# Moving the block differences of a two-stage MLP from GpSimd to VectorE, and giving the last token group its former first-stage order

## The chip, the cores and the metric

The kernel runs on one core of one Trainium2 chip. The metric is device time in microseconds (us), the median of three runs. Beside the runs there is one profiled execution, and every row of a trace in this document is from such an execution. The engines are PE (TensorE, matmul), PEld (its weight loads), DVE (VectorE), ACT (ScalarE), POOL (GpSimd) and SP (SyncE, which here issues nearly all DMAs).

## What is computed

```
scores = scale * q @ k.T - log(S)              # batch 8, 12 heads, S = 448, head size 64
attn   = 1 / (1 + exp(-scores))
x      = (attn @ v) as tokens x 768            # 3584 tokens
h      = x @ w_in                              # 768 x 2048
out    = relu(h)**2 @ w_out                    # 2048 x 768
```

Everything is float32 at the interface. The MLP behind the attention is the part that matters here.

## The kernel before

**Attention** runs first (to about 245 us of the span) and writes x to memory. The MLP then takes the 3584 tokens in four groups, g = 0 to 3. Groups 0, 1 and 2 hold 512 columns in each of two halves, group 3 holds 256 in each of two halves.

**Seven products.** Each group has two stages: the first multiplies by `w_in`, the second by `w_out`. Each matrix product is made from 2x2 blocks with seven block products instead of eight, so both operands are first combined by additions. The products are numbered 1 to 7. In the second stage they run one after the other in the order 1, 2, 6, 7, 5, 4, 3 (`ORDER`), each over eight positions i. In the first stage single steps (product, position) alternate, in an order that is a list: `LEAD` with the rest of `ROUNDS` behind it, then `TAIL`.

**Split operands.** A float32 operand is split into a high part (ACT copies it to the narrower type: line 379, tile names ending in h) and a low part (DVE subtracts the high part from the operand: line 381, names ending in l). A product of two split operands takes three matmuls: high x high, high x low, low x high. So ACT and then DVE stand before each operand of PE. Weights are loaded by SP into a pool of seven tiles (`w`), and a load waits until PE has used up the tile that it overwrites. A third of the last group's first-stage weights use other tiles (`spare`).

**Quartered products.** In groups 1 and 2 the products 2, 7 and 4 of the second stage (`TWICE`) are taken apart once more by the same scheme. For that each raw operand of 128x1024 (four pieces, j = 0 to 3, each with four blocks of 128x256) needs four *block differences*, t1, t3, t2, t4 (`differences_of`, lines 838 to 854). t2 needs t1, and t4 needs t2. For products 7 and 4 they overwrite the operand in place, for product 2 they go to a tile named d. They too are split: tiles d...h by ACT and d...l by DVE, and the split is placed `SPLIT_AFTER` steps later in the program. PE uses them in matmuls that write the banks oq (line 887).

**The order on each engine** is made by a scheduler when the program is built; each engine then runs its own list strictly in that order. An instruction that waits holds up all that stand behind it on its engine. PE does not pass over a matmul whose operand is late.

**The last group.** In group 3 the first stage takes the same list as the other groups (`STEPS[0]`), with about half the time for each step, because a step has 256 columns instead of 512. The operands of its products 7, 5, 3 and 4 are made during its own first steps:

```
EARLY_X = {0: (7,), 1: (5,), 3: (3,), 5: ("t4",), 6: (4,)}
...
            if m == 0 and 0 < g:
                for name in EARLY_X.get(at - sequence.index((g, 0, *order_of(g, 0)[0])), ()):
                    next_x[g - 1][name]()
```

In the first stage one PSUM bank takes the products 1, 6, 5 and 3 of a position one on top of the other (chain a). After product 1 and after product 6 ACT copies the bank (`snap`, line 754; tiles s1, s2), and the next product of that position must not write before the copy is done.

Of the kernel before, what the change touches and what calls it, by code (L numbers as in the profile page):

```python
# [15 lines left out]
ALU = mybir.AluOpType  # L16
# [12 lines left out]
NG = B // 2  # L29
# [11 lines left out]
NG = len(WIDTHS)  # L41
# [16 lines left out]
ROUNDS = [  # L58
    (n, j)
    for i in range(NI - 2)  # L60
    for n, j in ((1, i), (5, i - 1), (2, i), (6, i), (3, i - 1), (7, i), (4, i - 1))
    if 0 <= j
]
Y, Z = NI - 2, NI - 1
TAIL = [(1, Y), (5, Y - 1), (1, Z), (2, Y), (3, Y - 1), (2, Z), (4, Y - 1), (6, Y), (6, Z), (7, Y), (7, Z)]
TAIL += [(5, Y), (5, Z), (4, Y), (4, Z), (3, Y), (3, Z)]
LEAD = [(1, 0), (2, 0), (1, 1), (2, 1), (6, 0), (7, 0), (6, 1)]
LEAD += [(5, 0), (7, 1), (3, 0), (1, 2), (2, 2), (4, 0)]

STEPS = [LEAD + [s for s in ROUNDS if s not in LEAD] + TAIL]  # L70

BEHIND = {512: [(7, Y), (5, Y), (4, Y), (3, Y)], 256: [(7, Z), (4, Y)]}

# [9 lines left out]
    (3, 0): ("t3",),  # L83
}
EARLY_X = {0: (7,), 1: (5,), 3: (3,), 5: ("t4",), 6: (4,)}

ORDERS = [(n, i) for n in ORDER for i in range(NI)]
LAST = ORDER[-1], -1

TWICE = (2, 7, 4)  # L90
TWICE_IN = (1, 2)
SPLIT_AFTER = 5
Q = WIDE // 2
SUMS_AT = {2: (0, 0), 3: (0, 1), 4: (1, 0), 5: (1, 1), 1: (2, 0), 6: (2, 1), 7: (3, 0)}

# [13 lines left out]
def sigmoid_attention_relu2_mlp(  # L109
# [48 lines left out]
    nc = tc.nc  # L158
# [3 lines left out]
    def flat2(name, dtype=F32):  # L162
        return sb.tile([P, 2 * WIDE], dtype, tag="op2", bufs=N2, name=name)
# [214 lines left out]
    def split_to(hi, lo, raw, later=None):  # L378
        nc.scalar.copy(out=hi, in_=raw)  # L379
        if later is None:  # L380
            nc.vector.tensor_sub(out=lo, in0=raw, in1=hi.bitcast(F32))  # L381
        else:
            later.append(lambda: nc.vector.tensor_sub(out=lo, in0=raw, in1=hi.bitcast(F32)))
# [252 lines left out]

    def order_of(g, m):
        if m == 0:
            return STEPS[0]
        return ORDERS if g < NG - 1 else [*ORDERS[:-NI], LAST]  # L640

    sequence = [(g, m, n, i) for g in range(NG) for m in range(2) for n, i in order_of(g, m)]

    def units_of(g, m, n, i):
# [56 lines left out]
    spare = set()  # L701
    for at_unit, unit in enumerate(units):
        ahead, use = 0, first_use[unit]
        if unit[0] == NG - 1 and use >= sequence.index((NG - 1, 0, *STEPS[0][0])) + 4:
            ahead = 4
            if at_unit % 3 == 0:
                spare.add(unit)
        if at_unit >= READY:
            stream.setdefault(max(use - LOAD_AHEAD - ahead, 0), []).append((fetch, unit))
        if at_unit >= HALVED:  # L710
            stream.setdefault(max(use - HALVE_AHEAD - ahead // 2, 0), []).append((halve, unit))
        if unit[:2] == (0, 1):
            stream.setdefault(use - HALVE_AHEAD + KEEP_AFTER, []).append((keep, unit))
# [98 lines left out]
    def gemm2(g, blocks, operands1):  # L812
# [3 lines left out]
        ops, t2 = {1: operands1}, {}  # L816
# [3 lines left out]
        def operand(n, j):  # L820

            if n == 6:
                t2[j] = blocks_of(f"gt2_{g}_{j}", n_tok)
                nc.vector.tensor_sub(out=t2[j], in0=blocks["22", j], in1=blocks["12", j])
                raw = t2[j]
            elif n == 7:
                raw = blocks["11", j]
                nc.vector.tensor_sub(out=raw, in0=t2[j], in1=raw)
            elif n == 4:
                raw = blocks["21", j]  # L830
                nc.vector.tensor_sub(out=raw, in0=raw, in1=t2[j])
            else:
                raw = blocks[{2: "21", 5: "12", 3: "22"}[n], j]
            ops.setdefault(n, {})[j] = split_or_joint(raw, f"o{n}_{g}_{j}", n_tok)
            if n in twice:
                differences_of(n, j, raw)

        def differences_of(n, j, raw):

            name = f"d{n}_{g}_{j}"  # L840
            flat = raw.rearrange("p k s -> p (k s)")
            to = flat2(name) if n == 2 else flat
            b11, b12, b21, b22 = (flat[:, n * Q : n * Q + Q] for n in range(4))
            t1, t3, t4, t2 = (to[:, n * Q : n * Q + Q] for n in range(4))
            nc.gpsimd.tensor_tensor(out=t1, in0=b12, in1=b11, op=ALU.subtract)  # L845
            nc.gpsimd.tensor_tensor(out=t3, in0=b22, in1=b12, op=ALU.subtract)
            nc.gpsimd.tensor_tensor(out=t2, in0=b22, in1=t1, op=ALU.subtract)  # L847
            nc.gpsimd.tensor_tensor(out=t4, in0=b21, in1=t2, op=ALU.subtract)

            def parts():  # L850
                differences[n, j] = hi, lo = flat2(name + "h", F32R), flat2(name + "l", F32R)
                split_to(hi, lo, to)

            postponed.setdefault(now[0] + SPLIT_AFTER, []).append(parts)

# [181 lines left out]
    def run_steps(begin, end, between):  # L1037
        for at in range(begin, end):
            g, m, n, i = sequence[at]
            now[0] = at  # L1040
            if (m, n, i) == (0, *order_of(g, 0)[0]):
                made[g] = gemm1(g, ops[g])
            if (m, n, i) == (1, *ORDERS[0]):
                step, blocks, operands, done = made[g]
                done()
                second[g] = gemm2(g, blocks, operands)
            (second[g] if m else made[g][0])(n, i)
            for piece in between.get(at, []) + postponed.pop(at, []):
                piece()
            for piece, unit in stream.get(at, ()):  # L1050
                piece(unit)
            if m and g < NG - 1:
                if (n, i) == next(iter(NEXT_X)):
                    ops[g + 1], next_x[g] = x_operands(g + 1)
                for name in NEXT_X.get((n, i), ()):
                    next_x[g][name]()
            if m == 0 and 0 < g:
                for name in EARLY_X.get(at - sequence.index((g, 0, *order_of(g, 0)[0])), ()):
                    next_x[g - 1][name]()

    made, second, next_x, postponed, now = {}, {}, {}, {}, [0]

    with tc.manual_schedule():
# [46 lines left out]
        for n, piece in work:  # L1110
            between.setdefault(n, []).append(piece)
        run_steps(0, len(STEPS[0]), between)
    run_steps(len(STEPS[0]), len(sequence), {})


# [42 lines left out]
```

## Time and profile before

| what | value |
|---|---|
| median of 3 runs (lowest to highest) | 1064.69 us (1063.99 to 1065.31) |
| the profiled execution: its own time | 1063.85 us |
| its span, first to last instruction | 1062.1 us |
| PE busy | 1049.0 us, 99% |
| PEld busy | 819.9 us, 77% |
| DVE busy | 833.2 us, 78% |
| ACT busy | 689.0 us, 65% |
| POOL busy | 235.4 us, 22% |
| mean granted TensorE clock | 0.998 |

The span leaves out a little at both ends, which is why the execution's own time is 1.75 us longer. A share of busy time is a mean over stages that differ. A matmul's end is modelled in the profile, and neighbouring matmuls overlap, so the lost time of PE is better read from where a product starts and ends than from its busy share.

### The profile page before, as it was taken

The page shows a single profiled execution, that of the slowest core. Times are in us where ns is not written, and L with a number is a line of the kernel's source. Part 1 is how long each engine was busy: PE and PEld are TensorE (multiplying, and loading weights), DVE is VectorE, ACT ScalarE, POOL GpSimd, SP SyncE. Part 2 cuts the span into 40 slices and gives each one's busy share as a digit, 9 for nine tenths or more (in the row PEclk, how much of TensorE's full clock was granted, in tenths as well). Part 3 has the DMA queues.
Part 4 walks back from the last instruction along what each step waited for, and adds up shares of the span by engine and source line. Part 5 has one row for each costly group of instructions (what it writes and reads, how often), then busy time and mean ns, then how long its engine had stood idle before and what let it go on. Part 6 is the DMA issues. An engine that isn't in the chain of part 4 may idle for free.

```text
span 1062.1 us, 17197 instructions
## 1 busy us (share of the span) xinstructions
PE 1049.0 (99%) x6418; PEld 819.9 (77%) x6418; DVE 833.2 (78%) x1045; ACT 689.0 (65%) x960; POOL 235.4 (22%) x188
## 2 busy tenths in 40 slices
PE   9999999999999999999999998999999998999998
PEld 4555555557888888888888887888888887889987
DVE  6999998977768899796546788794556788958897
ACT  7998998877667855645444647564445646657873
POOL 1222231300222345300001537300003367200000
PEclk9999999999999999999999999999999999999999
DMA  9999999983666787993335877953337787856662
GB/s 366 404 394 368 337 405 361 326 300 111 214 215 208 242 275 249 326 325 114 97 104 175 275 270 241 350 153 92 89 97 244 240 311 256 264 174 180 204 198 85
DMA packets 121874, 255.93 MB, mean 241 GB/s; under 512 B 11712, under 2 KB 63680, under 8 KB 121792
## 3 DMA queue, kind: packets, MB, share of 16 engines
q1 hardware_dynamic: 121648, 254.79, 70.5%
q8 instruction: 50, 0.82, 0.3%
q14 instruction: 32, 0.26, 0.1%
q10 hardware_dynamic: 144, 0.07, 0.0%
HBM read 193.46 MB, written 61.34 MB: 240 GB/s over the span
## 4 chain that ended last, share of the span: by engine, by line
PE 90%; POOL 4%; DVE 3%; DMA 2%; ACT 1%; issue 0%; SPq 0%; ACTq 0%
PE ha L623 22%; PE oa L623 15%; PE pav L353 11%; PE hb L623 9%; PE sc L322 9%; PE hc L623 5%; PE ob L623 4%; PE oq L887 2%; PE oa L631 2%; PE oc L623 2%; PE sr L338 2%; PE pav L365 2%; POOL g L845 2%; DMA w<-w 1%; POOL g L847 1%; PE ob L631 1%
## 5 line engine op out<-in xcount | busy, mean ns | idle before, releaser
L381 DVE TENSOR_TENSOR w<-w 128x768 fp32r<-128x768 f32 (+1 forms) x164 | 148.9, 915 | 86.9 <-ACT w L379 75.2
L379 ACT CAST w<-w 128x768 fp32r<-128x768 f32 (+1 forms) x165 | 127.4, 781 | 95.7 <-DMA w<-w 85.5
L310 ACT ACTIVATE at<-sc 128x896 f32<-128x896 f32 x144 | 119.2, 941 | 3.0 <-PE sc L322 3.0
L353 PE MATMUL pav<-at,v 64*64 64x448 f32 x1152 | 118.1, 540 | 0.0
L353 PEld LDWEIGHTS pav<-at,v 64*64 64x64 f32 x1152 | 41.6, 133 | 60.8 <-issue 53.3
L212 POOL TENSOR_TENSOR a<-a,f 128x768 int32<-128x768 int32 x24 | 52.9, 2202 | 158.7 <-DVE a L209 82.9
L687 ACT CAST w<-w 128x768 fp32r<-128x768 f32 x56 | 46.7, 834 | 46.3 <-DMA w<-w 33.2
L754 ACT COPY s<-ha 128x512 f32<-128x512 f32 (+1 forms) x64 | 34.0, 533 | 65.2 <-PE ha L623 61.6
L845 POOL TENSOR_TENSOR d<-g 128x256 f32<-128x256 f32 x8 | 9.3, 1166 | 282.6 <-PE ha L623 136.5
L589 DVE TENSOR_TENSOR ql<-x,qh 128x896 fp32r<-128x896 f32 x46 | 67.9, 1516 | 0.0
L322 PE MATMUL sc<-qh 64*128 64x448 f32 x282 | 53.9, 379 | 0.0
L322 PE MATMUL sc<-ql,qh 64*128 64x448 f32 x282 | 51.3, 361 | 0.0
L322 PE MATMUL sc<-qh,ql 64*128 64x448 f32 x282 | 51.2, 360 | 0.0
L375 DVE TENSOR_TENSOR xo<-pav,xo 128x448 f32<-128x448 f32 x48 | 29.5, 621 | 24.5 <-ACT xo L371 24.3
L212 POOL TENSOR_TENSOR b<-b,fd 128x384 int32<-128x384 int32 x16 | 20.4, 1277 | 118.8 <-ACT w L379 56.9
L623 PE MATMUL oa<-o_0h,w 128*128 128x512 f32 x144 | 46.3, 389 | 0.0
L623 PE MATMUL oa<-o_1h,w 128*128 128x512 f32 x144 | 46.3, 389 | 0.0
L623 PE MATMUL oa<-o_2h,w 128*128 128x512 f32 x144 | 46.3, 389 | 0.0
L623 PE MATMUL oa<-o_3h,w 128*128 128x512 f32 x144 | 46.3, 389 | 0.0
L623 PE MATMUL ha<-x_0h,w 128*128 128x512 f32 x128 | 44.8, 390 | 0.0
L623 PE MATMUL ha<-x_2h,w 128*128 128x512 f32 x128 | 44.6, 389 | 0.0
L623 PE MATMUL ha<-x_1h,w 128*128 128x512 f32 x128 | 44.6, 389 | 0.0
(587 smaller groups left out, 3065.3 us busy)
## 6 DMA issues: line engine op xcount, KB each, us to landing
w<-w SPq DMA_DIRECT2D x193, 384.0 KB, 3.6
w<-h SPq DMA_DIRECT2D x56, 384.0 KB, 5.1
x<-qk SPq DMA_DIRECT2D x47, 448.0 KB, 6.3
f<-w_in SPq DMA_DIRECT2D x16, 768.0 KB, 8.6
v<-v SPq DMA_DIRECT2D x24, 448.0 KB, 6.9
xd<-xo SPq DMA_DIRECT2D x48, 224.0 KB, 4.9
h<-w SPq DMA_DIRECT2D x28, 384.0 KB, 4.3
w<-s SPq DMA_DIRECT2D x48, 192.0 KB, 7.3
```

The source lines that it names most:

```text
L212: nc.gpsimd.tensor_tensor(out=wb, in0=wb, in1=t.bitcast(I32)[:, :, 0], op=ALU.add)
L310: nc.scalar.activation(at, sc, AF.Sigmoid, bias=NEG_LOG_S, scale=SCALE)
L322: nc.tensor.matmul(sc[:, j], x[kp][rows, 1, ks], x[qp][rows, 0], start=(n == 0), stop=(n == len(passes) - 1),)
L353: nc.tensor.matmul(sums[columns, h], vt[rows, n % 2 * NT + t, columns], at[t][rows, j], start=(t == 0 and (n % 2, h) != (1, 1)), stop=(t = ...
L379: nc.scalar.copy(out=hi, in_=raw)
L381: nc.vector.tensor_sub(out=lo, in0=raw, in1=hi.bitcast(F32))
L589: nc.vector.tensor_sub(out=xs[n][1], in0=x[n], in1=xs[n][0].bitcast(F32))
L623: nc.tensor.matmul(out, a[:, c], b, start=first and n == 0, stop=last and n == 2, skip_group_check=True)
L631: nc.tensor.matmul(out, w[0][:, c], x, start=first, stop=False, skip_group_check=True)
L687: nc.scalar.copy(out=hi, in_=hi.bitcast(F32))
L754: nc.scalar.copy(out=s, in_=banks[chain, i])
L845: nc.gpsimd.tensor_tensor(out=t1, in0=b12, in1=b11, op=ALU.subtract)
```

## The change

Four things, in one edit. The four block differences are formed by DVE instead of GpSimd. Their split is placed two steps later in the program instead of five. The first stage of group 3 takes the list `ROUNDS + TAIL` (no `LEAD`). The operands of group 3's products 7, 5, 3 and 4 are made during product 3 of group 2's second stage (`LATE_X`) instead of during group 3's first steps.

```
-STEPS = [LEAD + [s for s in ROUNDS if s not in LEAD] + TAIL]
+STEPS = LEAD + [s for s in ROUNDS if s not in LEAD] + TAIL, ROUNDS + TAIL
...
+LATE_X = {(3, 1): (7,), (3, 3): (5,), (3, 5): (3,), (3, 6): ("t4",), (3, 7): (4,)}
...
-SPLIT_AFTER = 5
+SPLIT_AFTER = 2
...
-            return STEPS[0]
+            return STEPS[g == NG - 1]
...
-            nc.gpsimd.tensor_tensor(out=t1, in0=b12, in1=b11, op=ALU.subtract)
-            nc.gpsimd.tensor_tensor(out=t3, in0=b22, in1=b12, op=ALU.subtract)
-            nc.gpsimd.tensor_tensor(out=t2, in0=b22, in1=t1, op=ALU.subtract)
-            nc.gpsimd.tensor_tensor(out=t4, in0=b21, in1=t2, op=ALU.subtract)
+            nc.vector.tensor_sub(out=t1, in0=b12, in1=b11)
+            nc.vector.tensor_sub(out=t3, in0=b22, in1=b12)
+            nc.vector.tensor_sub(out=t2, in0=b22, in1=t1)
+            nc.vector.tensor_sub(out=t4, in0=b21, in1=t2)
...
-            if m == 0 and 0 < g:
+                for name in LATE_X.get((n, i), ()) if g == NG - 2 else ():
+                    next_x[g][name]()
+            if m == 0 and 0 < g < NG - 1:
```

What this does to DVE's list is seen at product 7 of group 1's second stage. Before, from the first split of product 7's operands on (o7 are those splits, d7 the splits of the differences, o5 the splits for product 5; the two digits behind are group and piece j, the last number a tile's own):

```order
L381 TENSOR_TENSOR o7_1_0l_6457<-g11_1_0_5312,o7_1_0h_6456 128x1024
L381 TENSOR_TENSOR o7_1_1l_6492<-g11_1_1_5480,o7_1_1h_6491 128x1024
L381 TENSOR_TENSOR o7_1_2l_6527<-g11_1_2_5699,o7_1_2h_6526 128x1024
L828 TENSOR_TENSOR g11_1_3_5906<-gt2_1_3_6408,g11_1_3_5906 128x1024
L381 TENSOR_TENSOR d7_1_0l_6544<-g11_1_0_5312,d7_1_0h_6543 128x1024
L831 TENSOR_TENSOR g21_1_1_5658<-g21_1_1_5658,gt2_1_1_6330 128x1024
L381 TENSOR_TENSOR o7_1_3l_6568<-g11_1_3_5906,o7_1_3h_6567 128x1024
L381 TENSOR_TENSOR d7_1_1l_6589<-g11_1_1_5480,d7_1_1h_6588 128x1024
L831 TENSOR_TENSOR g21_1_2_5851<-g21_1_2_5851,gt2_1_2_6371 128x1024
L381 TENSOR_TENSOR o5_1_0l_6623<-g12_1_0_5450,o5_1_0h_6622 128x1024
L831 TENSOR_TENSOR g21_1_3_6054<-g21_1_3_6054,gt2_1_3_6408 128x1024
L381 TENSOR_TENSOR d7_1_2l_6633<-g11_1_2_5699,d7_1_2h_6632 128x1024
```

The same place in the changed kernel, from the same split on (its lines count one more; 846 to 849 are the differences):

```order
L382 TENSOR_TENSOR o7_1_0l_6457<-g11_1_0_5312,o7_1_0h_6456 128x1024
L382 TENSOR_TENSOR o7_1_1l_6492<-g11_1_1_5480,o7_1_1h_6491 128x1024
L846 TENSOR_TENSOR g11_1_0_5312<-g11_1_0_5312 128x256
L846 TENSOR_TENSOR g11_1_1_5480<-g11_1_1_5480 128x256
L847 TENSOR_TENSOR g11_1_0_5312<-g11_1_0_5312 128x256
L847 TENSOR_TENSOR g11_1_1_5480<-g11_1_1_5480 128x256
L848 TENSOR_TENSOR g11_1_0_5312<-g11_1_0_5312 128x256
L848 TENSOR_TENSOR g11_1_1_5480<-g11_1_1_5480 128x256
L849 TENSOR_TENSOR g11_1_0_5312<-g11_1_0_5312 128x256
L849 TENSOR_TENSOR g11_1_1_5480<-g11_1_1_5480 128x256
L829 TENSOR_TENSOR g11_1_3_5906<-gt2_1_3_6408,g11_1_3_5906 128x1024
L382 TENSOR_TENSOR d7_1_0l_6500<-g11_1_0_5312,d7_1_0h_6499 128x1024
```

The differences of the pieces 0 and 1 now stand behind the second split, taken in turn. Those of the pieces 2 and 3 follow in the same way after four more splits (o7 and d7) and before the split d7 of piece 2. Three instructions of 128x1024 stand between the splits d7 of the pieces 2 and 3.

The other place is ACT's list where group 3 begins. Before, from the first copy of a bank in group 3 on (s1 and s2 are the copies after products 1 and 6, the digits behind are group and position; w0 are weights of the first stage: group, position, unit; x5 and x3 are operands of group 3):

```order
L754 COPY s1_3_0_9182<-ha_3_0_9172 128x256
L379 CAST x5_3h_9206<-x12_3_8852 128x768
L379 CAST w0_3_2_1_9204<-w0_3_2_1_9204 128x768
L754 COPY s1_3_1_9220<-ha_3_1_9210 128x256
L379 CAST x3_3h_9233<-x22_3_8854 128x768
L379 CAST w0_3_3_0_9262<-w0_3_3_0_9262 128x768
L754 COPY s2_3_0_9246<-ha_3_0_9172 128x256
```

The same place in the changed kernel, again from the first copy of a bank in group 3 on:

```order
L755 COPY s1_3_0_9205<-ha_3_0_9195 128x256
L380 CAST w0_3_2_0h_9168<-w0_3_2_0l_9169 128x768
L380 CAST w0_3_2_1_9219<-w0_3_2_1_9219 128x768
L755 COPY s2_3_0_9230<-ha_3_0_9195 128x256
L755 COPY s7_3_0_9239<-hb_3_0_9232 128x512
L380 CAST w0_3_3_0_9274<-w0_3_3_0_9274 128x768
L755 COPY s1_3_1_9253<-ha_3_1_9243 128x256
L380 CAST w0_3_2_2_9285<-w0_3_2_2_9285 128x768
```

The casts of x5 and x3 are gone from here (they stand earlier). The copy s2 of position 0 now stands behind the cast of `w0_3_2_1` and ahead of that of `w0_3_3_0`, and the copy s1 of position 1 stands behind the cast of `w0_3_3_0`.

## Rows read from the trace of the kernel before

**Rows 1.** The page's chain of waits: shares of the span by engine.

```profile
PE 90%; POOL 4%; DVE 3%; DMA 2%; ACT 1%; issue 0%; SPq 0%; ACTq 0%
```

**Rows 2.** Waits of PE: whom it waited for, total us, times, longest.

```profile
PE oq L887 <- DVE d_2l L381: 2.6, 2, 1.3
PE oq L887 <- ACT d_2h L379: 2.0, 2, 1.0
PE oq L887 <- DVE d_3l L381: 1.8, 2, 0.9
PE ha L623 <- ACT s L754: 1.7, 1, 1.7
...
PE oq L887 <- DVE d_1l L381: 0.6, 1, 0.6
```

**Rows 3.** PE's timeline, first matmuls of products; last: group 3's third step. Start, duration.

```profile
635.97 0.28 PE L887 MATMUL oq<-o_0h,w 128*128 128x256 f32 x1
...
656.19 0.39 PE L623 MATMUL oa<-o_0h,w 128*128 128x512 f32 x1
...
672.51 0.28 PE L887 MATMUL oq<-o_0h,w 128*128 128x256 f32 x1
...
705.24 0.39 PE L623 MATMUL ha<-x_2h,w 128*128 128x512 f32 x1
...
904.25 0.28 PE L887 MATMUL oq<-o_0h,w 128*128 128x256 f32 x1
...
936.17 0.28 PE L623 MATMUL ha<-x_3h,w 128*128 128x256 f32 x1
...
938.29 0.28 PE L623 MATMUL ha<-x_3h,w 128*128 128x256 f32 x1
```

**Rows 4.** Timeline of POOL: first and last of product 7's sixteen differences, group 1.

```profile
626.83 3.93 POOL L845 TENSOR_TENSOR g<-g 128x256 f32<-128x256 f32 x1 [23.37 <-DVE o_0l L381]
...
649.89 0.74 POOL L848 TENSOR_TENSOR g<-g 128x256 f32<-128x256 f32 x1
```

**Rows 5.** Timeline of ACT, product 7: in brackets idle time before, and releaser.

```profile
650.66 1.05 ACT L379 CAST d_3h<-g 128x1024 fp32r<-128x1024 f32 x1 [3.11 <-POOL g L848]
```

**Rows 6.** Timeline of DVE in group 1's second stage.

```profile
623.94 0.41 DVE L906 TENSOR_TENSOR qe<-oq,qe 128x256 f32<-128x256 f32 x1
624.27 0.41 DVE L911 TENSOR_TENSOR q<-q,qt 128x256 f32<-128x256 f32 x1
...
626.67 1.22 DVE L381 TENSOR_TENSOR o_1l<-g,o_1h 128x1024 fp32r<-128x1024 f32 x1
...
640.76 1.75 DVE L831 TENSOR_TENSOR g<-g,gt 128x1024 f32<-128x1024 f32 x1
...
661.30 0.42 DVE L905 TENSOR_TENSOR qt<-oq,qe 128x256 f32<-128x256 f32 x1
661.76 0.42 DVE L906 TENSOR_TENSOR qe<-oq,qe 128x256 f32<-128x256 f32 x1
...
675.66 1.22 DVE L436 TENSOR_TENSOR x<-x,x 128x1024 f32<-128x1024 f32 x1 [4.98 <-DMA x<-xd]
```

**Rows 7.** Windows, group 1's second stage: length; busy of PE, PEld, DVE, ACT, POOL.

```profile
588.00:704.00 116.00, 112.10 (x607) 96.68 (x606) 95.42 (x96) 70.81 (x87) 49.39 (x41) 1.00 0.79 267
```

**Rows 8.** Timeline of ACT at the start of group 3.

```profile
940.14 0.83 ACT L379 CAST w<-w 128x768 fp32r<-128x768 f32 x1 [1.60 <-issue]
...
944.35 0.83 ACT L379 CAST w<-w 128x768 fp32r<-128x768 f32 x1 [2.36 <-DMA w<-w]
945.09 0.37 ACT L754 COPY s<-ha 128x256 f32<-128x256 f32 x1
```

**Rows 9.** Timeline of SP: issue of the transfers that those two casts wait for.

```profile
936.36 0.33 SPq L284 DMA_DIRECT2D w<-w  x1
...
938.48 0.33 SPq L284 DMA_DIRECT2D w<-w  x1
```

**Rows 10.** Windows of 2 us behind: length, five busy times, granted clock, DMA share, GB/s.

```profile
946.00:948.00 2.00, 2.00 (x11) 1.81 (x10) 1.74 (x5) 2.00 (x5) 0.00 (x0) 0.53 0.16 63
948.00:950.00 2.00, 2.00 (x12) 1.90 (x11) 1.98 (x4) 1.18 (x3) 0.00 (x0) 0.61 0.00 0
```

More of the change, by code (lines that the diff above doesn't have):

```diff
@@ L703, in sigmoid_attention_relu2_mlp @@
         ahead, use = 0, first_use[unit]
-        if unit[0] == NG - 1 and use >= sequence.index((NG - 1, 0, *STEPS[0][0])) + 4:
+        if unit[0] == NG - 1 and use >= sequence.index((NG - 1, 0, *STEPS[1][0])) + 4:
             ahead = 4
```

## The prediction

> **What bounds the kernel now.** I read the chain of waits first. PE carries 90% of it, and POOL and DVE the most of what is left [rows 1]. So the kernel is a list of matmuls, and a change gains only what it takes away of PE's standing still. PE's waits say where that is [rows 2]: matmuls into the banks oq, which exist only in quartered products, wait for splits d_h and d_l of the block differences, and one wait of group 3's chain a is for ACT's copy of a bank. A row that counts two times is one wait in group 1 and one in group 2.
>
> How much time this is I take from where products begin, since a matmul's end is modelled [rows 3]. Product 7 of group 1 lasts 656.19 - 635.97 = 20.22 us. For an undisturbed quartered product I use group 2's products 4 and 3, which together last 936.17 - 904.25 = 31.92, and product 5 of group 1 (a plain product, as 3 is), 672.51 - 656.19 = 16.32. That leaves 31.92 - 16.32 = 15.60 for product 4, or 3.90 for each of four pieces. Product 7 therefore loses 20.22 - 15.60 = 4.62. Two groups: 9.24. Products 4 and 3 of group 1 last 705.24 - 672.51 = 32.73, so 0.81 is lost there, where DVE stood 4.98 us before an addition that waited for the DMA of an x tile [rows 6], with the split d_1l behind it in its list. [...] At those clocks the windows do 2 x 0.53 and 2 x 0.61 us of full-speed work, so 0.94 + 0.78 = 1.72 go too. In all 9.24 + 0.81 + 1.7 + 1.72 = 13.5 us stand to be won.
>
> **Why product 7 stalls.** POOL's sixteen differences for it start at 626.83 and end at 649.89 + 0.74 = 650.63, 23.8 us [rows 4]. ACT's cast d_3h has waited 3.11 us when the last one releases it, at 650.66 [rows 5]. Piece 3 is due at 635.97 + 3 x 3.90 = 647.67. PE arrives three to four us before its operand is made, and DVE still has to split it.
>
> **The differences on DVE.** Each quartered product takes 16 instructions of 128x256, 48 in a group, 96 in all. The trace has no such DVE instruction with all three tiles in SBUF, so I bound its price by neighbours of the same shape [rows 6]: independent ones begin 0.33 apart (623.94, 624.27), dependent ones 0.46 apart (661.30, 661.76). The new list takes two pieces in turn, so a result is mostly not needed by the next instruction: I take 0.36, nearer to the lower bound.
>
> Now product 7, rolled forward in the new order. DVE's second split began at 626.67 and lasts 1.22 [rows 6], to 627.9. Behind it: eight differences (2.6 to 3.7), five instructions of 128x1024 (6.1; beside POOL they take up to 1.75, but POOL has no differences any more), eight differences with one long instruction among them (3.8 to 4.9), ACT's cast d_2h (1.05 [rows 5]), then d_2l (1.22). That ends at 642.7 to 644.9, or 641.5 to 643.7 where the long instruction runs during ACT's cast. At 0.36 d_2l is there at about 642, before piece 2 is due (635.97 + 7.80 = 643.8). d_3l comes three long instructions and itself later (4.9), at about 647, just ahead of 647.7, and PE takes the low parts behind the first high ones. At both upper bounds together PE would wait about 1 us. What is late next in that case is DVE's splits o5 of product 5, which have their full product 7 to hide behind. So I give back the whole 4.62 per group.
>
> DVE's load over the second stage: 95.42 of 116 us are busy now [rows 7]. The differences add 48 x 0.33 = 15.8 to 48 x 0.46 = 22.1. Contention given back takes away between 0 and 30% ((1.75 - 1.22) / 1.75 [rows 6]) of POOL's 49.39 us [rows 7], 14.8. So DVE comes to between 96.4 and 117.5, and with 0.36 and half of the contention to 95.4 + 17.3 - 7.4 = 105.3, in a stage of 116 - 4.62 - 0.81 = 110.6. It fits, with 5 us spare; at the unfavourable ends it does not. For the 0.81 I count a full return, as the x operand's DMA is issued ahead of the output stores in the new order and the splits that stand behind it are those of product 3.
>
> [...]
>
> **Two steps later instead of five.** The split is now placed soon behind differences that DVE itself makes, so it waits only for ACT's cast. Cost nothing while DVE has other splits between (it has, three long ones); if that cover is gone, 1.05 us per piece.
>
> **Group 3's start.** Two steps last 938.29 - 936.17 = 2.12 us there [rows 3], one 1.06. Before, ACT's copy s2 of position 0 began at 945.09, right behind a cast that had waited 2.36 for its weights [rows 8], whose transfer SP issued at 938.48 [rows 9], 5.9 us before. In the new list s2 stands behind the cast of w0_3_2_1 instead, the one at 940.14 [rows 8], so it can start at about 941, before it is needed (five steps in, 941.5). What takes the place of that wait: s1 of position 1 now stands behind the cast of w0_3_3_0, and its bank is needed seven steps in, 943.6. With a transfer of 3.8 us (936.36 to 940.14 [rows 8, 9]) from an issue at about 938.5 the cast is there at 942.3, done at 943.1 and the copy (0.37) at 943.4: no wait. With 5.9 us it is 944.4 and some 1.9 us of wait, plus the clock again. The new list holds the following load back longer, so fewer transfers run beside it; I take 0.2. The x operands that leave this place are made beside product 3 of group 2, a plain product of 16.32 us with no differences to make; in the second stage of group 1 ACT is busy 70.81 and DVE 95.42 of 116 us [rows 7], so the room is there, and I count nothing. If it is not, x4 is late, which is used last.
>
> **Sum.** 13.5 - 0.2 = 13.3 us. The profiled execution's own time is 1063.85 (span 1062.1 and 1.75 at its ends); less 13.3 is 1050.55. The median of the runs, 1064.69, is 0.84 above the profiled execution, which gives 1051.4 in its terms. I take 1051.0.
>
> **Rivals.** **(A)** the forecast, 1051.0, own range 1050.0 to 1052.5; 0.58. **(B)** Group 3's wait is only moved, behind the cast of w0_3_3_0 (transfer 5.9 as before): 3.4 us stay, 1054.5. For it: the late transfer of [rows 8, 9]; against: fewer loads beside it. 0.18. **(C)** DVE becomes the bound of product 7 in part: differences at 0.46 and little contention returned. Between 1 us (the roll forward) and 6.9 us (117.5 - 110.6) per group, in the middle 4.6 over both, 1055.6. Against it: POOL's long spans vanish. 0.12. **(D)** Slower: DVE's list puts differences ahead of the splits o...l that PE needs first. A product's sixteen at 0.46 are 7.4 us, in six stages; if half lies bare, 22 us, and the time is 1063.85 - 13.3 + 22 = 1072.5. It decides from 13.3 / 6 = 2.2 us bare per stage on. Against it: product 7's operands o are split a whole product ahead of PE. 0.07. **(E)** No gain, 1064.7: DVE is slowed by as much as POOL was late. For it: a long instruction takes 1.75 instead of 1.22 beside POOL [rows 6], so the two engines share something. Against it: after the change POOL has nothing left to do there. [...] 0.05.
>
> **How the numbers follow.** A measurement of this kernel tells about 0.2%, 2.1 us, from no change. A, B and C are faster by more (0.88), E is the same (0.05), D slower (0.07). The range reaches from A's lower end, less 0.2 for the scatter of runs, over B to a little beyond C's middle, 1049.8 to 1056.0; outside lie D, E and C's far half.
>
> **What would show it.** Right: product 7 of groups 1 and 2 begins 15.6 us ahead of product 5, no oq wait is left, differences on DVE begin 0.33 to 0.46 apart, DVE's long instructions take 1.22 all through, DVE is busy about 105 us of the stage, and the windows at group 3's start have a granted clock of 1.00 with no ha wait. Wrong: oq waits for d_3l (C), an ha wait for s behind a cast of weights (B), or waits for o_l at the beginnings of quartered products (D).

## The result, and the profile after

| | before | changed |
|---|---|---|
| median of the runs (lowest to highest) | 1064.34 us (1062.60 to 1065.31), 4 runs (one more than in the first table) | 1052.79 us (1052.28 to 1053.76), 4 runs |
| the profiled execution's own time | 1063.85 us | 1052.28 us |
| its span | 1062.1 us | 1050.5 us |
| DVE busy; POOL busy | 833.2; 235.4 us | 843.8; 116.9 us |
| mean granted TensorE clock | 0.998 | 1.000 |

The ratio is 0.9894 with a 95% interval of 0.9877 to 0.9912: faster by 1.1%. The forecast was 1051.0 in a range of 1049.8 to 1056.0. In terms of the profiled execution it was 1050.55, and 1052.28 came, so 11.6 of the 13.3 us were won.

PE's waits in the changed kernel, as in [rows 2] (whom it waited for, total us, times, longest):

```profile
PE oa L632 <- DVE o_1j L382: 0.8, 1, 0.8
...
PE ha L624 <- ACT s L755: 0.4, 1, 0.4
```

The four rows of [rows 2] on the banks oq are gone altogether. Group 3's wait for s is 0.4 instead of 1.7, and a wait for o_1j has come that was not there before.

PE's timeline answers to [rows 3]: starts of product 7, 5 and 4 and of the next group's first stage in group 1, the beginning and end of product 7 and the beginning of product 4 in group 2, the start of group 3, and the two matmuls with a wait:

```profile
636.29 0.28 PE L888 MATMUL oq<-o_0h,w 128*128 128x256 f32 x1
...
651.89 0.39 PE L624 MATMUL oa<-o_0h,w 128*128 128x512 f32 x1
...
668.21 0.28 PE L888 MATMUL oq<-o_0h,w 128*128 128x256 f32 x1
...
700.13 0.39 PE L624 MATMUL ha<-x_2h,w 128*128 128x512 f32 x1
...
862.61 0.28 PE L888 MATMUL oq<-o_0h,w 128*128 128x256 f32 x1
...
878.21 0.39 PE L624 MATMUL oa<-o_0h,w 128*128 128x512 f32 x1
...
894.53 0.28 PE L888 MATMUL oq<-o_0h,w 128*128 128x256 f32 x1
...
926.45 0.28 PE L624 MATMUL ha<-x_3h,w 128*128 128x256 f32 x1
...
934.50 0.39 PE L624 MATMUL ha<-x_3h,w 128*128 128x256 f32 x1 [0.43 <-ACT s L755]
...
1039.17 1.33 PE L632 MATMUL oa<-o_1j,w 128*128 128x512 f32 x4 [0.81 <-DVE o_1j L382]
```

Product 7 lasts 651.89 - 636.29 = 15.60 us in group 1 and 878.21 - 862.61 = 15.60 in group 2. Products 4 and 3 last 700.13 - 668.21 = 31.92 in group 1 and 926.45 - 894.53 = 31.92 in group 2, which is the undisturbed length of [rows 3]. The second stage of both groups now runs without a gap.

DVE's timeline in product 7 of group 1: the second split, the first eight of the new differences (L846 to L849) and the two splits that PE had waited for:

```profile
627.29 1.22 DVE L382 TENSOR_TENSOR o_1l<-g,o_1h 128x1024 fp32r<-128x1024 f32 x1
628.43 0.75 DVE L846 TENSOR_TENSOR g<-g 128x256 f32<-128x256 f32 x2
629.10 0.75 DVE L847 TENSOR_TENSOR g<-g 128x256 f32<-128x256 f32 x2
629.77 0.75 DVE L848 TENSOR_TENSOR g<-g 128x256 f32<-128x256 f32 x2
630.44 0.76 DVE L849 TENSOR_TENSOR g<-g 128x256 f32<-128x256 f32 x2
631.12 1.22 DVE L829 TENSOR_TENSOR g<-gt,g 128x1024 f32<-128x1024 f32 x1
...
640.99 1.23 DVE L382 TENSOR_TENSOR d_2l<-g,d_2h 128x1024 fp32r<-128x1024 f32 x1 [0.29 <-ACT d_2h L380]
...
645.54 1.22 DVE L382 TENSOR_TENSOR d_3l<-g,d_3h 128x1024 fp32r<-128x1024 f32 x1
```

Eight differences take from 628.43 to 631.12, 2.69 us, so they begin 0.336 apart. d_2l is ready at 642.22 and d_3l at 646.76. In this execution product 7 begins at 636.29, so the pieces 2 and 3 are due at 644.09 and 647.99: margins of 1.9 and 1.2 us. Windows over group 1's second stage, as in [rows 7]:

```profile
588.00:700.00 112.00, 112.00 (x613) 97.69 (x613) 104.71 (x147) 72.27 (x89) 0.00 (x0) 1.00 0.82 281
```

DVE is busy 104.71 of 112 us, and POOL, 49.39 before, has nothing left to do.

The page's chain of waits, as in [rows 1], and then the piece of that chain behind which the wait for o_1j lies (start, us, what):

```profile
PE 92%; DVE 4%; ACT 1%; DMA 1%; issue 1%; SPq 0%; ACTq 0%; DVEq 0%
```

```profile
1008.53 5.25 DMA w<-w
...
1013.88 0.83 ACT w L380
...
1038.52 0.61 DVE o_1j L382
...
1039.17 1.33 PE oa L632 x4
```

From 985 us at the latest to 1039 the chain runs through ACT and DVE of the last group's second stage, not through PE. It contains a weight load of 5.25 us. In the kernel before the same load was issued at 1021.08 and its cast began at 1025.45, 4.37 us later; here it is 1008.53 and 1013.88, 5.35. Rows of before, from the timelines of SP, ACT, DVE and PE:

```profile
1021.08 0.43 SPq L284 DMA_DIRECT2D w<-w  x1
...
1025.45 0.83 ACT L379 CAST w<-w 128x768 fp32r<-128x768 f32 x1 [5.10 <-DMA w<-w]
...
1050.00 1.28 DVE L381 TENSOR_TENSOR o_1j<-g,o_1j 128x512 fp32r<-128x512 f32 x2
...
1050.90 0.40 PE L631 MATMUL oa<-o_1j,w 128*128 128x512 f32 x1
```

The first of the two o_1j was made from 1050.00 on in some 0.6 us (1.28 for both), for a matmul at 1050.90. So this place had about 0.3 us of slack before, and no row of PE's waits showed it.

### The profile page after: what moved, and what is told of

Its sections match the earlier page's. It is cut to its first block, busy times and chain, and to the rows that moved or that the text cites. A ratio compares the mean times of both kernels' runs of the same rounds, so it can differ in the third digit from the quotient of the medians.

```text
span 1050.5 us, 17173 instructions
## 1 busy us (share of the span) xinstructions
PE 1045.0 (99%) x6418; PEld 817.7 (78%) x6418; DVE 843.8 (80%) x1141; ACT 689.6 (66%) x960; POOL 116.9 (11%) x92
## 4 chain that ended last, share of the span: by engine, by line
PE 92%; DVE 4%; ACT 1%; DMA 1%; issue 1%; SPq 0%; ACTq 0%; DVEq 0%
PE ha L624 20%; PE oa L624 19%; PE pav L354 11%; PE hb L624 9%; PE sc L323 9%; PE oq L888 6%; PE ob L624 5%; PE hc L624 5%; PE oc L624 3%; PE sr L339 2%; PE pav L366 2%; DVE w L382 1%; DMA w<-w 1%; DVE o_0j L382 1%; PE hb L632 1%
## 5 line engine op out<-in xcount | busy, mean ns | idle before, releaser
L323 PEld LDWEIGHTS sc<-qh 64*128 64x128 f32 x282 | 26.4, 184 | 18.5 <-PE pav L354 16.2
L372 ACT COPY xo<-pav 128x448 f32<-128x448 f32 x48 | 25.5, 532 | 22.8 <-PE pav L366 11.1
```

What stands on the lines that cost most here:

```text
L323: nc.tensor.matmul(sc[:, j], x[kp][rows, 1, ks], x[qp][rows, 0], start=(n == 0), stop=(n == len(passes) - 1),)
```

## The experiments

Ratios are to the kernel before, with their 95% interval.

**Each part alone.** The differences (with the split two steps later) without group 3's order, and group 3's order without the differences.

```diff
 e1_diffs_only, against the kernel before
-            nc.gpsimd.tensor_tensor(out=t1, ...)     (all four)
+            nc.vector.tensor_sub(out=t1, ...)
-SPLIT_AFTER = 5
+SPLIT_AFTER = 2
 e2_group3_only, against the changed kernel
-            nc.vector.tensor_sub(out=t1, ...)        (all four)
+            nc.gpsimd.tensor_tensor(out=t1, ...)
-SPLIT_AFTER = 2
+SPLIT_AFTER = 5
```

> The kernel before with the differences on DVE and their split two steps later, group 3's first stage as before. Theory (the two parts add up, each removing its own waits): product 7 of both groups lasts 15.6 us, no wait in the banks oq, group 3's wait for the copy s2 stays at about 1.7 us with the low clock behind it. Against the changed kernel's profiled 1052.28 that is 3.5 - 0.7 = 2.8 us more, and 1.2 less if the wait for o_1j in the last group's second stage does not return: 1053.9 to 1055.1 us. Rival (group 3's wait was a consequence of the late second stage of group 2): 1052 us, no wait for s2. Rival (the two parts need each other): over 1056 us.

Measured: 1054.24 us (1053.50 to 1054.79), ratio 0.9904 (0.9890 to 0.9917). PE's waits have no row on oq, and keep group 3's:

```profile
PE ha L623 <- ACT s L754: 1.8, 1, 1.8
```

The differences do not need group 3's order, and group 3's wait does not come from the late second stage. Its price in this execution, though, was not the one I had put on it: the windows behind this wait, at 934 to 938 us, have a granted clock of 1.00, where those of [rows 10] had 0.53 and 0.61:

```profile
934.00:936.00 2.00, 0.21 (x2) 0.20 (x2) 0.49 (x1) 1.35 (x3) 0.00 (x0) 1.00 0.92 276
936.00:938.00 2.00, 2.00 (x15) 1.86 (x14) 1.74 (x4) 2.00 (x6) 0.00 (x0) 1.00 0.26 101
```

> The changed kernel with the differences back on GpSimd and their split five steps later: only group 3's order is changed. Theory: the waits in the banks oq are those of before (product 7 about 20.2 us), group 3's start loses 0.7 instead of 3.5, so 1063.85 - 2.8 = 1061.0 us, and 1062.2 if the wait for o_1j in the last stage comes as well. Rival (group 3's order is worth nothing by itself): 1063.9 us.

Measured: 1065.18 us (1062.50 to 1066.66), ratio 1.0002 (0.9992 to 1.0011). Alone this part is worth nothing that can be told; the theory missed and the rival held. In the profiled execution, whose own time of 1062.9 us is among the lowest of its eleven, PE waits 0.8 us for s instead of 1.7. The low clock is there all the same, now behind the waits of product 7 in group 2 (windows of 2 us; the granted clock is the third number from the end):

```profile
880.00:882.00 2.00, 1.50 (x7) 1.50 (x8) 1.96 (x2) 0.45 (x1) 1.92 (x2) 0.53 0.95 350
882.00:884.00 2.00, 2.00 (x11) 1.95 (x11) 0.11 (x1) 0.46 (x1) 1.43 (x2) 0.61 0.02 8
```

There it cost nothing that can be seen: group 2's second stage lasts 937.30 - 820.69 = 116.61 us with it, and 936.17 - 819.48 = 116.69 in the kernel before without it. PE waits for operands that come at GpSimd's pace in both (by the rows of PE's waits over groups 1 and 2, d_2l 2.6 and d_2h 2.0 us in either kernel). Why the median of the eleven runs shows no gain stays open.

**GpSimd's pace, or the place of the splits?** The two halves of the other part.

```diff
 e3_split5, against the changed kernel
-SPLIT_AFTER = 2
+SPLIT_AFTER = 5
 e4_pool_split2, against the changed kernel
-            nc.vector.tensor_sub(out=t1, ...)        (all four)
+            nc.gpsimd.tensor_tensor(out=t1, ...)
```

> The changed kernel with SPLIT_AFTER 5 instead of 2, differences still on DVE. Theory (GpSimd's pace was the cause, the place of the splits is not): by DVE's new list d_2l of product 7 ends at about 642.9 and d_3l at 646.8, before they are due, so no oq wait and 1052.3 us within 1 us. Rival (the earlier split is what removed the waits): several us in product 7 or 4 of both groups, 1056 us and more.

Measured: 1052.32 us (1051.33 to 1054.05), ratio 0.9886 (0.9870 to 0.9902): the changed kernel's time, no wait on oq.

> The changed kernel with the differences on GpSimd, but their split two steps later. Theory (GpSimd's pace): sixteen differences still take over 20 us, product 7 still loses 4 to 6 us in each group, and DVE is now held up at the splits earlier in its list: 1061 to 1065 us. Rival (the place of the splits did it): 1052.5 us.

Measured: 1064.02 us (1061.98 to 1065.02), ratio 0.9995 (0.9986 to 1.0004). PE waits on oq for d_1, d_2 and d_3 as before. POOL's timeline has the first and the last difference of product 7 here:

```profile
630.12 3.93 POOL L846 TENSOR_TENSOR g<-g 128x256 f32<-128x256 f32 x1 [23.74 <-DVE o_0l L382]
...
651.33 1.60 POOL L849 TENSOR_TENSOR g<-g 128x256 f32<-128x256 f32 x1
```

They still take 22.8 us. So the earlier split is worth nothing on either engine, and GpSimd's pace is what was removed.

**What GpSimd beside VectorE costs, and how much room VectorE has.**

```diff
 e8_ghost, against the changed kernel (behind the four differences; idle is a tile added for this)
+            lo = ops[n][j][1].rearrange("p k s -> p (k s)")[:, :Q].bitcast(F32)
+            for first in (lo, idle, idle, idle):
+                nc.gpsimd.tensor_tensor(out=idle, in0=first, in1=idle, op=ALU.subtract)
 e9_double, against the changed kernel (ahead of the four differences; idle as above)
+            for _ in range(4):
+                nc.vector.tensor_sub(out=idle, in0=b12, in1=b11)
```

> The changed kernel, and beside it GpSimd again does four subtractions of 128x256 for each set of differences, on a tile of its own whose result nobody waits for (the first of each four reads the split o_l, so that they run at about the former place). So GpSimd's beat beside VectorE is back, its lateness is not. Theory (DVE's instructions beside GpSimd took up to 1.75 instead of 1.22, and the change gave this back): DVE's long instructions are at 1.5 to 1.75 there, the split d_3l of product 7 comes 4 to 7 us later, PE waits 3 to 5.5 us for it in each group, 1058 to 1064 us. Rival (only GpSimd's lateness mattered): 1052 to 1053.5 us.

Measured: 1073.76 us (1070.49 to 1074.37), ratio 1.0071 (1.0048 to 1.0093): 21 us above the changed kernel and slower than the kernel before. The direction was the theory's, the size was not. PE waits for d_3l in all three quartered products of both groups, which is the first row of its waits:

```profile
PE oq L894 <- DVE d_3l L385: 11.3, 6, 2.9
PE ha L627 <- ACT s L758: 1.6, 2, 1.1
PE oq L894 <- DVE d_2l L385: 1.2, 2, 0.9
```

DVE's timeline at product 7, and POOL's over the same stretch:

```profile
647.34 1.22 DVE L835 TENSOR_TENSOR g<-g,gt 128x1024 f32<-128x1024 f32 x1
...
649.30 1.27 DVE L385 TENSOR_TENSOR d_2l<-g,d_2h 128x1024 fp32r<-128x1024 f32 x1 [0.41 <-ACT d_2h L383]
650.49 1.63 DVE L835 TENSOR_TENSOR g<-g,gt 128x1024 f32<-128x1024 f32 x1
652.04 1.63 DVE L385 TENSOR_TENSOR o_0l<-g,o_0h 128x1024 fp32r<-128x1024 f32 x1
...
655.15 1.74 DVE L385 TENSOR_TENSOR d_3l<-g,d_3h 128x1024 fp32r<-128x1024 f32 x1
```

```profile
635.72 13.77 POOL L855 TENSOR_TENSOR idle<-o_0l,idle 128x256 f32<-128x256 f32 x1 [21.57 <-DVE o_0l L385]
649.57 4.58 POOL L855 TENSOR_TENSOR idle<-idle 128x256 f32<-128x256 f32 x3
```

Once POOL's instructions run, DVE's long ones begin 1.55 us apart (650.49 to 652.04) instead of 1.13, and over the whole span DVE is busy 879.2 us instead of 843.8 with as many instructions. The change therefore did two things in one: it made the operands earlier, and it took away GpSimd's drag on the engine that now makes them. The second is not a by-product: with as many subtractions left on GpSimd the move loses 9 us against the kernel before (1073.76 against 1064.36; some of that is low clock: the mean granted clock is 0.98 in each of the windows 588 to 700 and 814 to 926, against 1.00 in the changed kernel).

> The changed kernel, and before each set of four differences DVE does four more subtractions of 128x256 whose result nobody uses, so that the differences cost it twice as much. Price by the trace of the changed kernel: 0.335 apart, 48 x 0.335 = 16.1 us more in each of two second stages of 110.6 us, in which DVE was busy for about 104. Theory (DVE has about 6 us to spare in a stage): 10 us are missing in each, 1064 to 1076 us, with waits for d_l and o_l in the quartered products. Rival (DVE's load has much room, only its order counts): under 1057 us.

Measured: 1055.00 us (1054.03 to 1057.41), ratio 0.9908 (0.9890 to 0.9927). 32 us more work on DVE cost 2.2 us by the medians. The theory, 10 us lost in each of two second stages, falls. One reason is that it put all 48 extra subtractions of a group there: by the trace the 16 for product 2 run in the first stage ahead of it, and 32, or 32 x 0.336 = 10.7 us, in the second. Windows over group 1's second stage and the first stage of group 2, each from the stage's first matmul to the next one's, of this kernel and then of the changed one:

```profile
589.91:704.51 114.60, 112.91 (x613) 97.77 (x612) 109.01 (x172) 72.99 (x90) 0.00 (x0) 1.00 0.79 271
704.51:819.06 114.55, 114.55 (x505) 94.52 (x504) 76.97 (x100) 52.20 (x77) 0.00 (x0) 1.00 0.43 131
```

```profile
588.05:700.13 112.08, 112.08 (x613) 97.77 (x612) 104.84 (x147) 72.35 (x89) 0.00 (x0) 1.00 0.82 281
700.13:814.37 114.24, 114.24 (x505) 94.59 (x504) 64.59 (x77) 51.43 (x76) 0.00 (x0) 1.00 0.42 126
```

In the second stage DVE is busy only 4.2 us more than without the extra work (109.01 against 104.84), in the first stage that follows 12.4 us more (76.97 against 64.59), of which 16 extra subtractions for group 2 are 5.4. So some 7 us of work that is not due yet moved on into a stage where DVE has 40% to spare: DVE's list does not end with the stage. The room is not free, though. In this execution, the longest of its four runs (1057.41 us), group 1's second stage lasts 114.60 instead of 112.08 us and group 2's 932.68 - 819.06 = 113.62, and PE waits again:

```profile
PE oq L892 <- DVE d_1l L384: 1.6, 2, 1.3
PE oq L892 <- ACT d_2h L382: 1.0, 2, 0.7
```

**What is left: two loads.**

```diff
 e5_store_pool, against the changed kernel (in put, the last group's stores that add a snapshot)
-                    (falls through to nc.sync.dma_start)
+                    nc.gpsimd.dma_start(out=to, in_=o)
+                    return
 e6_lead_late, against the changed kernel
-            return STEPS[g == NG - 1]
+            return STEPS[0]
...
-        if unit[0] == NG - 1 and use >= sequence.index((NG - 1, 0, *STEPS[1][0])) + 4:
+        if unit[0] == NG - 1 and use >= sequence.index((NG - 1, 0, *STEPS[0][0])) + 4:
```

> The changed kernel; the output stores of the last group's second stage that add a snapshot are issued by GpSimd, which has nothing else to do there, instead of SP. Theory (the wait for o_1j near the end, 1.2 us in the profile, comes from a weight load that stands behind these stores in SP's list and then shares the transfers with them): that load is issued over 1 us earlier, the wait is gone, and 1052.28 becomes about 1051.1 in the profiled execution; the medians differ by 0.5 to 1.2. Rival (the load waits for its tile, not for the stores): 1052.3, no change.

Measured: 1055.00 us (1054.01 to 1056.49), ratio 0.9906 (0.9890 to 0.9921). The wait for o_1j is gone, as the theory said. It is gone too in the profiles of e11 and e12 below, which issue these stores the same way; of the nine other profiles that make group 3's operands early and leave the stores on SP, seven have it, with 0.2 to 0.8 us. The time is not less, and there the theory missed. In the profiled execution group 3's wait is 2.5 us:

```profile
PE ha L624 <- ACT s L755: 2.5, 1, 2.5
```

> The changed kernel with the former list (LEAD) for group 3's first stage, while the operands of group 3 are still made during product 3 of group 2. Theory (the order of the first stage's steps decides behind which cast the copy stands): a wait for the copy s2 of about 2 us returns, 1053.5 to 1054.5 us. Rival (the casts of the operands x5 and x3 held the copy up): no wait at group 3's start, 1051.5 to 1052.3 us.

Measured: 1054.19 us (1053.42 to 1055.68), ratio 0.9899 (0.9883 to 0.9915). The wait for s is back at 1.8 us: the order of the steps decides it, not the casts of x5 and x3.

Three more kernels try to remove both waits, beside the changed kernel once more.

```diff
 e10_later_ahead, against the changed kernel
-        if unit[0] == NG - 1 and use >= sequence.index((NG - 1, 0, *STEPS[1][0])) + 4:
+        if unit[0] == NG - 1 and use >= sequence.index((NG - 1, 0, *STEPS[1][0])) + 8:
 e11_later_stores: e10 and the edit of e5
 e12_more_stores: e10 and
-            nc.sync.dma_start(out=to, in_=o)
+            (nc.gpsimd if g >= NG - 2 else nc.sync).dma_start(out=to, in_=o)
```

> The changed kernel once more, beside the next three. Theory (what is left varies with two weight transfers): group 3's wait is the transfer of w0_3_3_0 less about 3.9 us (it was 0.57, 0.69, 0.99, 1.9 and 2.6 us in five profiles with transfers of 4.48, 4.50, 4.89, 5.81 and 6.52), the wait for o_1j near the end 0.2 to 1.2; 1052 to 1054 us.

> The changed kernel; only the weights that are used from the ninth step of group 3 on (before: from the fifth) are loaded and split four and two steps earlier. By this the copy s1 of position 1 stands behind the cast of w0_3_2_1, and the cast of w0_3_3_0 behind that copy. Theory (the transfer of w0_3_3_0 holds the copy up): no wait that follows that transfer; w0_3_2_1 is issued about 1 us after group 3's start and is there at 5 to 7, so 0 to 0.7 us of wait instead of 0.6 to 2.6; 0.5 to 1.5 us less than the changed kernel beside it. Rival (another load is late in its place): no gain.

> The former and the output stores of the last stage on GpSimd's queue together. Theory: both waits gone, 1 to 2.5 us less than the changed kernel beside it, 1050.5 to 1051.5 us. Rival (GpSimd's queue costs elsewhere what it saves): not less than the kernel of the former experiment.

> As the former, but all stores of that kind of groups 2 and 3 go to GpSimd's queue, so that SP's loads at group 3's start do not stand behind the last stores of group 2 either. Theory: w0_3_2_1 is issued about 1 us earlier and no wait is left at group 3's start; 1050 to 1051.2 us. Rival (the loads wait for their tiles, not for the stores): the same as the former.

Measured: 1053.49 us (1052.56 to 1054.09) for the changed kernel, 1053.38 (1052.91 to 1053.65), 1055.62 (1052.75 to 1055.87) and 1052.99 (1052.20 to 1054.99) for the three. None is clearly better than the changed kernel, none of the three comes as low as its theory had it, and no version here is claimed to beat it. What nine profiles with the new order show together is the cause of group 3's wait (e8 and e9 have the new order too, but other copies stand ahead of these casts on ACT there). At 2.3 us after group 3's first matmul SP issues a weight load, and the copy s of position 1 stands behind its cast. In the changed kernel:

```profile
928.77 0.33 SPq L285 DMA_DIRECT2D w<-w  x1
...
933.34 0.83 ACT L380 CAST w<-w 128x768 fp32r<-128x768 f32 x1 [1.43 <-DMA w<-w]
934.08 0.37 ACT L755 COPY s<-ha 128x256 f32<-128x256 f32 x1
```

| profile | issue to cast, us | PE's wait for s, us |
|---|---|---|
| e12_more_stores | 934.99 - 930.89 = 4.10 | none at this place |
| e3_split5 | 934.97 - 930.41 = 4.56 | 0.41 |
| the changed kernel | 933.34 - 928.77 = 4.57 | 0.43 |
| e10_later_ahead | 935.28 - 930.71 = 4.57 | 0.43 |
| after_again | 935.46 - 930.64 = 4.82 | 0.67 |
| e2_group3_only | 944.59 - 939.62 = 4.97 | 0.83 |
| e4_pool_split2 | 945.86 - 939.97 = 5.89 | 1.75 |
| e11_later_stores | 936.08 - 929.68 = 6.40 | 2.3 |
| e5_store_pool | 935.80 - 929.21 = 6.59 | 2.5 |

The wait is the transfer less 4.1 us in every row, within 0.1. The transfer varies by 2.5 us over the table, and by 2.0 between executions whose instructions up to there are the same (the changed kernel, after_again and e5). In e10 another load, that of w0_3_2_1, came to stand at this place and took as long: its rival held.

e12 has neither wait, and its group 3 lasts 1051.1 - 928.53 = 122.57 us instead of the changed kernel's 1050.5 - 926.45 = 124.05. The gain is lost elsewhere. Group 1's first stage lasts 587.73 - 473.50 = 114.23 us in the kernel before and 587.98 - 473.74 = 114.24 in e1, but 588.05 - 473.40 = 114.65 in the changed kernel and 114.7 to 116.3 in the eleven other profiles, in e12 590.13 - 473.84 = 116.29. In ten of the eleven PE waits there 0.4 to 1.0 us for an instruction of DVE, in e12:

```profile
PE ha L624 <- DVE g L759: 1.0, 1, 1.0
```

The lists of ACT, DVE and SP in that stage are the same before and after the change. Whether the rest of the new order costs this time, or executions just differ, one profile of each kernel cannot tell.

## Why the prediction was right, step by step

**Product 7 and products 4 and 3.** 4.62 twice and 0.81 were forecast, and all came: 15.60 and 31.92 us in both groups. The reason given for the 0.81 held too: the addition of the x tile, before which DVE stood 4.98 us, begins at 671.18 without a wait. e1 has this part alone at 10.2 us by the medians (1064.4 in its comparison, and 1054.24), against 9.24 + 0.81 = 10.05. The cause, GpSimd's pace, is shown by e4 (back on GpSimd, the waits are back) and e3 (the place of the split is worth nothing).

**Price on DVE.** 0.336 apart, between the bounds of 0.33 and 0.46 and nearly the lower, where I took 0.36. d_2l and d_3l were forecast at about 642 and 647 and came at 642.22 and 646.76. That this agrees so well is in part luck: from DVE's second split, where the roll forward began, they were put 642 - 626.67 = 15.3 and 20.3 us later and came 642.22 - 627.29 = 14.9 and 19.5 later, while that split itself began 0.6 us later than before. The duration of one by itself is 0.42 us, as for the neighbours of [rows 6]; what the engine pays is the spacing, 2.69 us for eight. VectorE did not become the bound: no row of PE's waits on oq is left.

**The range.** Rival C was summed wrongly. Between 1 and 6.9 us per group the middle is 3.95, so 7.9 over both and 1058.9 us, not 4.6 and 1055.6. The range's upper end of 1056.0 stood short of it. C did not come, so the forecast does not hang on this.

**Contention given back.** I took half of 14.8 us; DVE's 104.71 against the forecast 105.3 fits that. But I had it as a correction to a load, and e8 shows that it carries the result. Rival E, that DVE is slowed by as much as POOL was late, came and more where GpSimd stayed busy (e8: POOL 61.19 us of the window 588 to 700, 1073.76 us against 1064.36); it did not come where GpSimd fell idle (0.00 us in that window of the changed kernel, 1052.79 us).

**DVE's room.** The step "It fits, with 5 us spare; at the unfavourable ends it does not" came to the right end by a measure that is too strict. e9 puts DVE's sum at 104.84 + 10.7 = 115.5 us for a second stage of 112.08, 3.4 over, and the two stages get 2.5 and 1.5 us longer in its profiled execution; by the medians it loses 2.2 in all. Rival D's price (half of the work bare, 22 us) was too high by the same error: what counts is each operand's due time, and DVE's other work can slip into the next stage.

**Group 3's start.** 3.22 us were forecast (1.7 + 1.72 - 0.2: PE's wait for s in [rows 2]; what the granted clocks of 0.53 and 0.61 in the two windows of [rows 10] take from 4 us; and the wait that I expected in its place). In the profiled execution group 3's first stage lasts 986.86 - 926.45 = 60.41 us instead of 999.57 - 936.17 = 63.40, so 2.99 came. By the medians the part is worth about 1 us between e1 (1054.24) and the changed kernel (1052.79 and 1053.49), whose ranges overlap, and nothing in e2. So this term was mis-sized, in two parts. The clock's 1.72 us was counted as certain to come back, but it is not tied to this wait: e1 has the wait without the low clock, e2 has the low clock elsewhere, and at this place e11 has a granted clock of 0.50 behind its wait of 2.3 us (window 938 to 940; 0.998 in the mean of that execution) where e5 has 1.00 behind one of 2.5 (1.000 in the mean). And for the load that takes the wait's place I took the 3.8 us of one transfer [rows 8, 9] and 0.2 us of wait; it is 4.1 to 6.6, and 0 to 2.5. Six of the nine are under 5 us, against 5.9 for the load that was waited for before; three are not. That is rival B in part: the mechanism that it named, at 0.4 us in the profiled execution and 1.75 to 2.5 in three others. The reason for the 0.2, fewer transfers beside it, was my estimate and is not what the traces show: in the changed kernel SP issues the next load (w_3l) 929.15 - 928.77 = 0.38 us behind the load that takes the wait's place, behind the one waited for in the kernel before it came 940.61 - 938.48 = 2.13 us later.

**What no step had.** The last group's second stage, where DVE was only 0.3 us ahead of PE before. PE was ready for o_1j at 1039.17 - 0.81 = 1038.36, 12.5 us earlier than before (1050.90), but DVE's chain behind the slower load was only 11.5 us earlier (1038.52 against 1050.00), and PE waits. e5 takes this wait away by issuing the stores elsewhere. The profiled execution missed its forecast by 1.7 us. By the lengths of the stages 1.1 of it lies here (group 3's second stage lasts 1050.5 - 986.86 = 63.6 us instead of 1062.1 - 999.57 = 62.5, of which the wait is 0.81), 0.2 at group 3's start and 0.4 in group 1's first stage, whose cause is open.

## What to carry to other kernels

Before a small operation is moved to a busier engine, take its spacing there, not its duration (here 0.336 and 0.42 us), and roll the list forward to the moment each operand is due: that came within 0.9 us here over 20, while the sum of busy time over a stage put a price of some 7 us on e9's extra work where 2 to 4 were paid. Where work goes from GpSimd to VectorE, look at what stays on GpSimd beside it: in e8 it slowed the engine that now has the work, from 1.22 to 1.63 us for a long instruction. When a gain of 1% is in sight, ask which chain is only just ahead of the bounding engine, and read the transfers on it from several profiles, since one profile gives one draw of them (here 4.1 to 6.6 us for one load). And compare the lengths of all stages, not only of those that the change was meant for.

## What the hardware showed that was not expected

GpSimd and VectorE did not simply slow each other. In e8 POOL's first subtraction is listed from 635.72 for 13.77 us; in that time DVE ran without a gap, at 1.22 for each long instruction, until it stood 0.41 us before 649.30. Only from then on did POOL go forward, and DVE's long instructions took 1.63. In group 2 it is listed for 16.04 us, until DVE's first gap, of 0.10 us, before 888.46. The kernel before has the same, shorter: POOL's first difference takes 3.93 us from 626.83 [rows 4], while DVE's three long instructions from 626.67 on run at 1.21 to 1.22 each without a gap to 630.16; then DVE stands for 4.16 us, and POOL's next three take 0.73 to 0.74. So at these three places a VectorE without gaps held GpSimd off over several instructions, and in e8, once GpSimd was in, they went on in turn, one POOL instruction (1.53 apart) to one DVE instruction (1.55 apart). The spans on POOL are rough; DVE's own durations bear this out. That the two contend is what the traces show; through what, and why POOL waited as long as eleven of DVE's long instructions of 1.22, no run here shows.
